# Fourier and MoE kernel on one core: the second transform's fold moved behind its product for the second batch, and its result stores moved from SyncE's queue to ScalarE's

## The chip, the cores and the metric

The kernel runs on one core of a Trainium2 chip. The metric is device time in microseconds (us) of the whole program; what is compared is the median over runs. A profiled execution records every instruction of each engine: PE (TensorE's matmuls), PEld (its weight loads), DVE (VectorE), ACT (ScalarE), POOL (GpSimd), and SPq (the DMA instructions that SyncE issues).

## The reference

Everything is computed on two batches of 3136 rows by 256 columns.

```python
def _attn_ref(x, w_r, w_i, b_r, b_i):
    X = np.fft.rfft(x, axis=1)
    Yr = Xr @ w_r - Xi @ w_i + b_r          # Xr, Xi: real and imaginary part
    Yi = Xr @ w_i + Xi @ w_r + b_i
    # soft threshold by 0.01 on both, then the inverse transform
    return np.fft.irfft(Y, n=x.shape[1], axis=1)

def _moe_ref(x, g_ln, w_ch1, w_ch2):        # 256 -> 1024 -> 256
    xn = (x - mu) / np.sqrt(var + 1e-06) * g_ln
    return x + np.maximum(xn @ w_ch1, 0.0) @ w_ch2

def _moe2_ref(x, w_ch1, w_ch2):
    mixed = np.real(np.fft.fft(np.fft.fft(x, axis=1), axis=2))
    u = x + mixed
    un = (u - mu) / np.sqrt(var + 1e-06)    # no gain
    return u + np.maximum(un @ w_ch1, 0.0) @ w_ch2
```

The kernel's output is `_moe2_ref(_moe_ref(_attn_ref(x)))`.

## The kernel before, in words

Products that need accuracy are made of three passes: each operand is split into a rounded high part and the remainder (low part), and high times high, high times low and low times high are added up in PSUM. Splitting costs a copy (the high part) and a subtraction (the low part) on ACT, DVE or POOL.

**Stages in time.** The first transform and its inverse fill the first part. Then 12 chunks of the first MLP (`mlp1`) run, and then 13 chunks of the second (`mlp2`), each of up to 512 rows. A chunk loads its rows (L591), normalises them (`prep`, L605 to L622: statistics on DVE, and for the chunks that the change touches, the two passes of the normalisation on ACT, four instructions of L621 and four of L622), transposes them on PE (L636 into a `psc` tile), copies them out as high and low part (L641 or L202 on ACT, L642 or L210 on DVE), and then runs two layers. Layer 1 is eight tiles of six matmuls (L220 to L222 into `psa`), each drained by one ACT instruction (L660, the ReLU and high part) and one DVE instruction (L661, the low part); `psa` has 3 buffers. Layer 2 is four tiles of sixteen matmuls (L677, L678 into `psb`, 2 buffers), each drained by two DVE additions (L681, L682) and then stored (L690). PE runs layer 1 of a chunk, then layer 2, with the transposes of the next chunk before the last layer 2 tile.

**The second transform** is the class `Stage98`. It works along the rows of one batch in 16 steps, on a 98x512 piece each. Its object for batch 0, `s4[0]`, is woven into chunks 8 to 10 of `mlp1` (about 350 to 425 us), its object for batch 1, `s4[1]`, into chunks 0 to 3 of `mlp2` (about 492 to 607 us). A step loads a piece that is wanted two steps later (L350), splits another into high and low part, multiplies (L220 to L222 into `psc`, 3 buffers), and copies the result into one of 4 slots of a ring `o98`, from where it is stored to the scratch tensor `dA2` in DRAM (L425). A slot is written again only when its store has landed. `mlp2` reads `dA2` back (L725, L727).

Along the columns the second MLP's transform needs, for each column c and its mirror image, the sum and the difference of the two: the *fold*. For batch 0 the fold is done behind the product: ACT copies columns 0 to 127 out of PSUM (98x256), ACT copies two middle columns from the tile `mid`, and DVE writes difference (L420) and sum (L421). For batch 1 the fold is done ahead of the product, on the loaded piece: three POOL instructions (L369 to L371) write the folded piece `w`, ACT copies its high part `s` (L202, 98x512), POOL subtracts (L210), and after the product ACT copies the whole tile (98x512) and POOL the two middle columns (L424). The loaded pieces lie in a ring `t98` of 2 for batch 0 and in a ring `r98` of 4 for batch 1.

**What sets the order.** The program text gives a priority by position, hooks (`STAGE4_AT`, `STAGE4_MLP2`) say behind which tile of which chunk a step of `Stage98` is written, and a scheduler orders the instructions of each engine with an estimate of when each is ready. On the chip each engine then runs its own list strictly in order, and waits on semaphores at the head. All loads and stores stand in SP's list.

Of the kernel before, what the change touches and what calls it, by code (L numbers as in the profile page):

```python
# [162 lines left out]
def fourier_moe_kernel(ctx, tc, x, w_r, w_i, b_r, b_i, g_ln, w11, w12, w21, w22,  # L163
                       t_ca, t_cam, t_cim, t_cb, t_ci, t_cb0, t_ci0, t_cd, t_ident, out):
    nc = tc.nc
    sp = nc.sync
# [8 lines left out]
    def psum(tag):  # L175
        return pp.tile([128, 512], F32, tag="ps" + tag, name="ps" + tag, bufs=ps_bufs[tag])
# [24 lines left out]
    def a_copy(o, i, scale=1.0):  # L201
        nc.scalar.activation(out=o, in_=i, func=AF.Copy, scale=scale)  # L202
# [15 lines left out]
    def mm3r(ps, lh, ll, rh, rl, first, last):  # L218

        nc.tensor.matmul(out=ps, lhsT=lh, rhs=rh, start=first, stop=False)  # L220
        nc.tensor.matmul(out=ps, lhsT=ll, rhs=rh, start=False, stop=False)  # L221
        ins = nc.tensor.matmul(out=ps, lhsT=lh, rhs=rl, start=False, stop=last)  # L222
        mark["pe"] = getattr(ins, "ins", ins)


    def scratch(nm):
        return [dp.tile([NQ, FW], F32, name=f"{nm}{b}") for b in range(NB)]

    dY, dX1, dA2 = (scratch(n) for n in ("dY", "dX1", "dA2"))
# [48 lines left out]
    class Forward:  # L278


        def __init__(self, b, tag, slot):
            self.b, self.tag, self.slot = b, tag, slot
            self.raw = {}
            self.g = 0
# [10 lines left out]
        def step(self):  # L295
            g = self.g
            if g >= 16:
                return
            e = g % 2
            ps = psum(self.tag)  # L300
            nc.tensor.matmul(out=ps, lhsT=cam, rhs=self.raw[g // 2][:, e * 512:(e + 1) * 512], start=True, stop=True)  # L301
            ins = nc.vector.transpose(out=yg[self.b].rearrange("p k c -> p c k")[:, g * 16:(g + 1) * 16, :],
                                      in_=ps.rearrange("p (c j) -> p c j", j=32))
            mark["dve"] = getattr(ins, "ins", ins)
            self.g += 1
# [28 lines left out]
    class Stage98:  # L334
# [3 lines left out]
        def __init__(self, src, dst, ch, cl, tag):  # L338
            self.src, self.dst, self.ch, self.cl, self.tag = src, dst, ch, cl, tag
            self.raw, self.hl = {}, {}  # L340
            self.fold_last = src is dX1[0]
            self.g = self.nl = self.ns = 0

        def load(self):
# [58 lines left out]
        def step(self):  # L403
            g = self.g
            if g >= 16:
                return
            if g == 0:
                self.middle2()
            self.load()
            self.split()  # L410
            h, l = self.hl.pop(g)
            ps = psum(self.tag)
            mm3r(ps[0:NQ, :], self.ch, self.cl, h, l, True, True)
            o = next(o98_ring)[0:NQ]
            if self.fold_last:
                v, w = (a.rearrange("q (j c) -> q j c", c=D) for a in (ps[0:NQ, :], o))
                a_copy(w[:, :, 0:128], v[:, :, 0:128])
                a_copy(w[:, :, 128], self.mid[:, 2 * g:2 * g + 2])
                lo, hi = w[:, :, 1:128], v[:, :, 255:128:-1]
                nc.vector.tensor_tensor(out=w[:, :, 129:256], in0=lo, in1=hi, op=ALU.subtract)  # L420
                nc.vector.tensor_tensor(out=lo, in0=lo, in1=hi, op=ALU.add)  # L421
            else:
                a_copy(o, ps[0:NQ, :])
                nc.gpsimd.tensor_copy(o[:, 128:512:256], self.mid[:, 2 * g:2 * g + 2])  # L424
            sp.dma_start(out=self.dst[:, g * 512:(g + 1) * 512], in_=o)  # L425
            self.g += 1


# [587 lines left out]
```

## Time and profile before

| what | value |
|---|---|
| median of 3 runs | 822.34 us (822.14 to 823.64) |
| the profiled execution's own time | 823.36 us |
| its span in the profile | 821.5 us |
| granted TensorE clock, share of full speed | 0.998 |
| PE busy | 806.9 us (98%) |
| DVE busy | 534.1 us (65%) |
| ACT busy | 304.5 us (37%) |
| POOL busy | 122.9 us (15%) |

The span is the time from the first to the last recorded instruction; 1.9 us of the execution's own time lie outside it. The profiled execution took 1.02 us more than the median of the runs. A busy share is a mean over stages, so a wait is looked up where it stands, in the timeline of its engine.

In a timeline each row has the start, the time that the instruction (or a row of `xN` like ones) took, the engine, the line, the operation, the tile it writes and the tiles it reads, and in brackets how long the engine had been idle before it and which instruction ended that wait. Successive matmuls overlap in the pipe, so a matmul that is listed with 0.40 us is followed by the next one after about 0.23 us.

### The profile page before, as it was taken

To read this page: it belongs to the slowest core of one execution; us is meant where nothing else is said; L and a number is where in the kernel's file an instruction comes from. 1 tells how busy PE (TensorE), PEld (TensorE's weight loads), DVE (VectorE), ACT (ScalarE), POOL (GpSimd) and SP (SyncE) were. 2 spreads that over 40 slices of the span, in tenths; PEclk is the share of its full clock that TensorE was granted. 3 is DMA by queue.
4 is the path that set the end of the run, shared out by engine and by line. 5 is a ranking of instruction groups with operands and counts; after the bars stand their busy time and mean duration, and the time that the engine had idled before them with its cause. 6 is when DMAs were issued, how large, how long until landed. Compare 5 with 4: busy or idle time off the path is not lost.

```text
span 821.5 us, 12201 instructions
## 1 busy us (share of the span) xinstructions
PE 806.9 (98%) x4456; PEld 674.9 (82%) x4456; DVE 534.1 (65%) x1268; ACT 304.5 (37%) x637; POOL 122.9 (15%) x154
## 2 busy tenths in 40 slices
PE   9999999999999999999999999999999999999996
PEld 3888977967878889978888887888888898888885
DVE  6479996475666588956558655645655667655653
ACT  1422356353344222353442224555632233332221
POOL 1222221211000000045400004635300000000000
PEclk9999999999999999999999999999999999999999
DMA  8742200621015301354333113343232221210001
GB/s 225 217 136 88 78 1 2 214 101 51 2 52 171 118 35 68 123 143 154 98 108 97 63 52 84 118 141 98 90 89 84 58 62 56 65 52 26 20 16 29
DMA packets 48175, 71.57 MB, mean 87 GB/s; under 512 B 11746, under 2 KB 32490, under 8 KB 47920
## 3 DMA queue, kind: packets, MB, share of 16 engines
q1 hardware_dynamic: 48116, 70.80, 28.2%
q8 instruction: 35, 0.57, 0.3%
q14 instruction: 24, 0.20, 0.1%
HBM read 45.09 MB, written 25.69 MB: 86 GB/s over the span
## 4 chain that ended last, share of the span: by engine, by line
PE 85%; DVE 6%; DMA 5%; SPq 1%; POOL 1%; issue 1%; ACT 1%; ACTq 0%; POOLq 0%
PE psb L677 22%; PE psb L678 11%; PE psa L220 11%; PE psa L222 11%; PE psa L221 11%; PE psb L480 4%; PE psc L320 3%; PE psc L741 3%; PE psc L636 3%; PE psc L301 2%; PE psc L500 2%; DMA cb<-in_cb_dram 1%; PE psa L766 1%; PE psa L448 1%; DMA h<-in_x_dram 1%; PE psc L220 1%
## 5 line engine op out<-in xcount | busy, mean ns | idle before, releaser
L660 ACT ACTIVATE h<-psa 128x512 fp32r<-128x512 f32 (+2 forms) x208 | 117.1, 573 | 238.8 <-PE psa L222 213.7
L661 DVE SCALAR_TENSOR_TENSOR h<-psa,h 128x512 fp32r<-128x512 f32 (+2 forms) x208 | 134.4, 654 | 81.6 <-ACT h L660 79.8
L677 PE MATMUL psb<-r2b,h 128*128 128x512 f32 x392 | 138.0, 399 | 0.0
L677 PE MATMUL psb<-r3a,h 128*128 128x512 f32 x392 | 137.6, 399 | 0.0
L678 PE MATMUL psb<-r3a,h 128*128 128x256 f32 x392 | 106.2, 281 | 0.0
L678 PE MATMUL psb<-r2b,h 128*128 128x256 f32 x392 | 105.8, 280 | 0.0
L480 PE MATMUL psb<-wm,h 128*128 128x256 f32 (+1 forms) x600 | 88.8, 298 | 0.7 <-DVE w L486 0.7
L681 DVE TENSOR_TENSOR o<-psb,yb 128x256 f32<-128x256 f32 x74 | 30.1, 422 | 85.9 <-PE psb L678 85.7
L677 PEld LDWEIGHTS psb<-r3a,h 128*128 128x128 f32 x392 | 71.9, 188 | 16.0 <-PE psa L222 0.3
L677 PEld LDWEIGHTS psb<-r2b,h 128*128 128x128 f32 x392 | 71.9, 188 | 15.0
L480 PEld LDWEIGHTS psb<-wm,h 128*128 128x128 f32 (+1 forms) x600 | 76.1, 189 | 8.5 <-issue 8.0
L220 PE MATMUL psa<-q,r3a 128*128 128x512 f32 (+2 forms) x208 | 82.7, 398 | 0.3 <-ACT q L641 0.2
L220 PE MATMUL psa<-q,r2b 128*128 128x512 f32 (+2 forms) x208 | 82.4, 396 | 0.5 <-ACT q L202 0.3
L221 PE MATMUL psa<-q,r3a 128*128 128x512 f32 (+2 forms) x208 | 78.7, 378 | 0.0
L221 PE MATMUL psa<-q,r2b 128*128 128x512 f32 (+2 forms) x208 | 78.5, 378 | 0.0
L222 PE MATMUL psa<-q,r2b 128*128 128x512 f32 (+2 forms) x208 | 78.2, 380 | 0.0
L222 PE MATMUL psa<-q,r3a 128*128 128x512 f32 (+2 forms) x208 | 78.1, 380 | 0.0
L678 PEld LDWEIGHTS psb<-r3a,h 128*128 128x128 f32 x392 | 73.9, 189 | 4.2 <-issue 1.0
L678 PEld LDWEIGHTS psb<-r2b,h 128*128 128x128 f32 x392 | 74.0, 189 | 2.9
L202 ACT ACTIVATE yg<-psc 98x512 f32<-98x512 f32 (+2 forms) x58 | 48.5, 860 | 56.7 <-PE psc L500 27.8
L210 POOL TENSOR_TENSOR h<-w 128x512 f32<-128x512 f32 (+1 forms) x26 | 34.5, 1327 | 109.6 <-DVE w L487 70.4
L220 PEld LDWEIGHTS psa<-q,r3a 128*128 128x128 f32 x208 | 39.1, 188 | 9.5 <-DVE h L661 1.3
(115 smaller groups left out, 1230.9 us busy)
## 6 DMA issues: line engine op xcount, KB each, us to landing
s<-in_moe_w_ch_dram SPq DMA_DIRECT2D x16, 512.0 KB
r<-dX SPq DMA_DIRECT2D x32, 196.0 KB
dA<-o SPq DMA_DIRECT2D x32, 196.0 KB
dY<-yg SPq DMA_DIRECT2D x12, 512.0 KB
r<-dA SPq DMA_DIRECT2D x48, 128.0 KB
dX<-o SPq DMA_DIRECT2D x11, 512.0 KB
yb<-dX SPq DMA_DIRECT2D x50, 64.0 KB
out_dram<-o SPq DMA_DIRECT2D x50, 64.0 KB
```

Of the source, the lines that this page charges most:

```text
L202: nc.scalar.activation(out=o, in_=i, func=AF.Copy, scale=scale)
L210: ins = eng.tensor_tensor(out=o, in0=a, in1=b, op=ALU.subtract)
L220: nc.tensor.matmul(out=ps, lhsT=lh, rhs=rh, start=first, stop=False)
L221: nc.tensor.matmul(out=ps, lhsT=ll, rhs=rh, start=False, stop=False)
L222: ins = nc.tensor.matmul(out=ps, lhsT=lh, rhs=rl, start=False, stop=last)
L320: nc.tensor.matmul(out=ps[0:NQ, :], lhsT=cim, rhs=t, start=True, stop=True)
L480: nc.tensor.matmul(out=ps[0:m, u * D:(u + 1) * D], lhsT=xv[:, o:o + m], rhs=wm_hl[wv][:, e, c, :], start=k == 0, stop=k == 11)
L660: nc.scalar.activation(out=h[:, 0:n], in_=ps[:, 0:n], func=AF.Relu)
L661: ins = nc.vector.scalar_tensor_tensor(out=l[:, 0:n], in0=ps[:, 0:n], scalar=0.0, in1=h[:, 0:n], op0=ALU.max, op1=ALU.subtract)
L677: nc.tensor.matmul(out=ps, lhsT=h[:, ts_], rhs=w2[:, f, :], start=f == 0, stop=False)
L678: nc.tensor.matmul(out=ps[:, 0:D], lhsT=l[:, ts_], rhs=w2[:, f, 0:D], start=False, stop=f == NF - 1)
L681: nc.vector.tensor_tensor(out=o, in0=ps[:, 0:D], in1=self.y[:, i, :], op=ALU.add)
```

## The change

For batch 1 the fold goes behind the product as it is for batch 0 (the flag `fold_last` holds for both objects). With that its load goes to the ring of 2 (`t98`), its split becomes a POOL cast (L361) and a POOL subtraction (L210), and its result is made by ACT's copy of 98x256, ACT's copy of two middle columns, L420 and L421 on DVE. And all 32 result stores (L425), those of batch 0 too, are issued by ACT instead of SP.

```diff
         def __init__(self, src, dst, ch, cl, tag):
             self.src, self.dst, self.ch, self.cl, self.tag = src, dst, ch, cl, tag
             self.raw, self.hl = {}, {}
-            self.fold_last = src is dX1[0]
+            self.fold_last = True
             self.g = self.nl = self.ns = 0
...
                 nc.gpsimd.tensor_copy(o[:, 128:512:256], self.mid[:, 2 * g:2 * g + 2])
-            sp.dma_start(out=self.dst[:, g * 512:(g + 1) * 512], in_=o)
+            nc.scalar.dma_start(out=self.dst[:, g * 512:(g + 1) * 512], in_=o)
             self.g += 1
```

The first place is ACT's list where batch 1 begins, in chunk 0 of `mlp2`. `s` is the high part of a piece, `w` the folded piece that POOL writes, `mid` the middle columns. Before:

```order
L660 ACTIVATE h<-psa 128x512
L202 ACTIVATE s_1657<-w 98x512
L660 ACTIVATE h<-psa 128x512
L202 ACTIVATE s_1657<-w 98x512
L610 ACTIVATE sm<-mv,e_81 128x4
L202 ACTIVATE ng<-mv 128x4
L621 ACTIVATE q<-yb,ng 128x256 x4
L202 ACTIVATE s_1657<-w 98x512
L622 ACTIVATE q<-q,sm 128x256 x4
L202 ACTIVATE mid<-psc 98x32
```

After the change the same place reads:

```order
L660 ACTIVATE h<-psa 128x512 x2
L610 ACTIVATE sm<-mv,e_81 128x4
L202 ACTIVATE ng<-mv 128x4
L621 ACTIVATE q<-yb,ng 128x256 x4
L622 ACTIVATE q<-q,sm 128x256 x4
L202 ACTIVATE mid<-psc 98x32
L202 ACTIVATE o_1658<-mid 98x2 x4
L202 ACTIVATE q<-psc 128x512 x2
```

The three copies `s<-w` between the last ReLUs (L660) of chunk 0 and the normalisation (L621, L622) of chunk 1 are gone from ACT's list, the normalisation follows the ReLUs directly, and four copies of middle columns stand behind `mid`.

The second place is ACT's list in chunk 9 of `mlp1`, where the normalisation of chunk 10 stands among the last ReLUs of chunk 9; `dA_70` is the scratch tensor of batch 0, `o_1658` the ring of 4 slots. Before:

```order
L660 ACTIVATE h<-psa 128x512
L621 ACTIVATE q<-yb,ng 128x256 x4
L660 ACTIVATE h<-psa 128x512
L622 ACTIVATE q<-q,sm 128x256 x4
L660 ACTIVATE h<-psa 128x512
L202 ACTIVATE o_1658<-mid 98x2 x2
L202 ACTIVATE o_1658<-psc 98x2x128
L660 ACTIVATE h<-psa 128x512
L202 ACTIVATE o_1658<-mid 98x2
L202 ACTIVATE o_1658<-psc 98x2x128
```

After the change:

```order
L660 ACTIVATE h<-psa 128x512
L621 ACTIVATE q<-yb,ng 128x256 x4
L425 DMA dA_70<-o_1658 98x512 x2
L660 ACTIVATE h<-psa 128x512
L622 ACTIVATE q<-q,sm 128x256 x4
L660 ACTIVATE h<-psa 128x512
L202 ACTIVATE o_1658<-mid 98x2
L202 ACTIVATE o_1658<-psc 98x2x128
L202 ACTIVATE o_1658<-mid 98x2
L660 ACTIVATE h<-psa 128x512
L425 DMA dA_70<-o_1658 98x512
L202 ACTIVATE o_1658<-mid 98x2
```

Three store issues now stand among these rows, two together ahead of a ReLU (L660) and the third straight ahead of a copy into the ring; before the change they stood in SP's list. Of the two middle copies that stood together, one now stands behind the 98x256 copy. In the whole of ACT's list after the change, 16 of the 29 rows of stores stand straight ahead of an L660 row. PE's list is the same in both kernels up to this chunk, and has the same number of matmuls in all.

## Rows read from the trace of the kernel before

**Rows 1.** The page: the chain that ended last, by engine, share of the span.

```profile
PE 85%; DVE 6%; DMA 5%; SPq 1%; POOL 1%; issue 1%; ACT 1%; ACTq 0%; POOLq 0%
```

**Rows 2.** One stretch: its length, busy PE, PEld, DVE, ACT, POOL (instructions), clock, DMA.

```profile
500.00:550.00 50.00, 48.29 (x266) 40.52 (x265) 24.97 (x62) 26.66 (x60) 24.09 (x40) 1.00 0.40 117
```

**Rows 3.** Timeline of PE from 497 to 506.

```profile
497.04 0.39 PE L222 MATMUL psa<-q,r2b 128*128 128x512 f32 x1
...
502.65 0.40 PE L678 MATMUL psb<-r2b,h 128*128 128x256 f32 x2
504.76 0.44 PE L636 MATMUL psc<-ident,q 128*128 128x128 f32 x2 [1.71 <-ACT q L622]
...
505.75 0.48 PE L677 MATMUL psb<-r2b,h 128*128 128x512 f32 x1
```

**Rows 4.** Timeline of ACT, 496 to 506.

```profile
496.10 0.60 ACT L660 ACTIVATE h<-psa 128x512 fp32r<-128x512 f32 x1 [0.41 <-PE psa L222]
499.40 0.63 ACT L202 ACTIVATE s<-w 98x512 fp32r<-98x512 f32 x1 [2.71 <-POOL w L371]
499.94 0.58 ACT L660 ACTIVATE h<-psa 128x512 fp32r<-128x512 f32 x1
...
501.87 1.71 ACT L621 ACTIVATE q<-yb,ng 128x256 f32<-128x256 f32 x4
503.68 0.63 ACT L202 ACTIVATE s<-w 98x512 fp32r<-98x512 f32 x1
504.21 1.69 ACT L622 ACTIVATE q<-q,sm 128x256 f32<-128x256 f32 x4
```

**Rows 5.** Timeline of POOL, the same stretch.

```profile
497.82 0.73 POOL L369 TENSOR_TENSOR w<-r 98x254 f32<-98x254 f32 x1 [0.53 <-DMA r<-dX]
...
500.83 1.31 POOL L210 TENSOR_TENSOR s<-w,s 98x512 fp32r<-98x512 f32 x1
```

**Rows 6.** Timeline of DVE, the same stretch.

```profile
500.55 0.69 DVE L661 SCALAR_TENSOR_TENSOR h<-psa,h 128x512 fp32r<-128x512 f32 x1 [2.11 <-ACT h L660]
```

**Rows 7.** Timeline of PE, chunk ends at 534 and 594.

```profile
534.63 1.24 PE L636 MATMUL psc<-ident,q 128*128 128x128 f32 x6
535.63 0.48 PE L677 MATMUL psb<-r2b,h 128*128 128x512 f32 x1
...
594.53 1.04 PE L636 MATMUL psc<-ident,q 128*128 128x128 f32 x8
595.32 0.47 PE L677 MATMUL psb<-r2b,h 128*128 128x512 f32 x1
```

**Rows 8.** Instructions on the tile o: count, ns min/median/max, first and last start.

```profile
L202 ACT ACTIVATE o<-psc x32: 364/492/601, 359.1 to 601.9; 98x256 f32<-98x256 f32 x16, 98x512 f32<-98x512 f32 x16
L425 SPq DMA_DIRECT2D dA<-o x32: 307/314/2858, 363.4 to 604.2; - x32
...
L202 ACT ACTIVATE o<-mid x16: 188/202/208, 353.0 to 414.0; 98x2 f32<-98x2 f32 x16
L420 DVE TENSOR_TENSOR o<-o,psc x16: 382/410/422, 361.5 to 422.9; 98x254 f32<-98x254 f32 x16
...
  DMA dA<-o: 15.6, 7
```

**Rows 9.** Timeline of SP around 370 (a store) and 604.

```profile
369.52 0.31 SPq L425 DMA_DIRECT2D dA<-o  x1
...
604.20 2.86 SPq L425 DMA_DIRECT2D dA<-o  x1
```

**Rows 10.** Timeline of ACT around 372.

```profile
371.81 0.21 ACT L202 ACTIVATE o<-mid 98x2 f32<-98x2 f32 x1 [3.40 <-DMA dA<-o]
```

**Rows 11.** Timeline of DVE around 374.

```profile
374.20 0.75 DVE L682 TENSOR_TENSOR o<-psb,o 128x256 f32<-128x256 f32 x2
```

**Rows 12.** Timeline of PE around 374.

```profile
374.76 0.47 PE L677 MATMUL psb<-r3a,h 128*128 128x512 f32 x1
```

**Rows 13.** Timeline of ACT at the end of batch 0's steps.

```profile
417.64 0.60 ACT L660 ACTIVATE h<-psa 128x512 fp32r<-128x512 f32 x1 [1.01 <-PE psa L222]
```

## The prediction

> **What bounds the kernel now.** I read the chain that ended last first: 85% of it is PE, and ACT and POOL together are 2% [rows 1]. So an edit on ACT, POOL, DVE or SP moves the time only where it ends a wait of PE. The second view is busy time by stretch, over the stretches in which batch 1's steps run: PE is busy 48.29 of the 50 us from 500 to 550 [rows 2], so there is one hole of 1.71 us. The third is PE's timeline there: the hole stands whole before the transposes of chunk 1, at 504.76, and was ended by ACT's L622 [rows 3]. Then ACT, POOL and DVE in the same stretch, to see why L622 was late. Last come the instructions on the result tile `o`, whose issues the change moves, and the timelines where they stand on tight places.
>
> **Why L622 is late.** The last tile of layer 1 of chunk 0 was started on PE at 497.04 [rows 3]. ACT should drain it with L660. But ahead of that L660 stands a copy `s<-w`, which waited 2.71 us for POOL's fold [rows 4]; POOL began that fold when the load had landed, at 497.82 [rows 5]. L660 started at 499.94, DVE's L661 behind it had waited 2.11 us and ran at 500.55 [rows 4, 6]. The statistics of chunk 1 stand behind L661, and the normalisation starts at 501.87, that is 1.32 us after L661 did [rows 4, 6]. Between its two passes a third `s<-w` stands: L621 starts at 501.87 and takes 1.71, L622 starts at 504.21, 0.63 of that being the copy [rows 4].
>
> **The fold, step by step.** The three `s<-w` leave ACT's list (first pair of pieces of the order), so L660 can run when its tile is complete, about 497.04 + 0.39 = 497.43 plus a hand-over. I take 497.45 to 498.05 with its 0.60 [rows 4]. DVE's L661 follows from about 498.45, since two statistics instructions of the next chunk stand ahead of it; that is 2.1 us earlier than 500.55. With the same 1.32 us behind it L621 starts at 499.77, L622 at about 501.4, and its first result is there 0.55 us later (504.21 to 504.76), at 501.95. PE comes to the transposes at 504.76 - 1.71 = 503.05. The cover is 1.1 us, and the hole goes: -1.71. What is late next? The fourth L622 ends at 501.4 + 1.69 = 503.1, when PE is only at its first transposes. The split of the first two pieces is two casts (I take half of the subtraction's 1.31 for each) and two subtractions on POOL: 497.82 + 1.3 + 2.6 = 501.7 [rows 5], ahead of the products, which stand behind the transposes. So nothing takes the hole's place.
>
> At two later chunk ends the same copies stand between L621 and L622, and the transposes are stretched without a gap being shown: from their first to the next layer 2 matmul 535.63 - 534.63 = 1.00 us, against 595.32 - 594.53 = 0.79 where there is no `s<-w` left [rows 7]. 564 looks like 534. L622 will start 0.6 us earlier there: -0.21 twice, -0.4.
>
> What the fold adds lies beside PE. DVE gets 32 instructions of 0.41, 13.1 us, over the 100 us in which it was about half busy (24.97 of 50) [rows 2, 8]. ACT's result copy gets shorter (0.36 for 98x256 by the minimum of the row, 0.6 for 98x512 by its maximum) and gains a 0.20 copy, so those two cancel [rows 8]; 16 `s<-w` of 0.63, 10 us, go. POOL loses work and is on no path. I take nothing for these, with -0.3 to +0.6 us as ends. The upper: two fold instructions ahead of the L661 of a late tile make it 0.8 late, most of which three `psa` buffers swallow; I give 0.2 at each of three chunk ends. The lower: ACT's ReLUs come earlier wherever an `s<-w` stood ahead of them, half of the 0.63 at one place where PE waits.
>
> **The stores on ACT.** On SP an issue took 307 to 2858 ns, median 314 [rows 8]. That ACT's issue costs the same is not shown by any row; I take 0.31, with 0 and 2.9 as ends. 32 of them are 10 us more on ACT, as much as the fold takes off it. But an issue waits at the head of ACT's list for DVE's L421, and behind it stand ReLUs: in 16 of 29 places the next row is an L660. On SP behind it stood loads of pieces for the splits, which had time; these get free, and since only POOL waits for them I give nothing for it. Three kinds of place pay:
>
> (a) Chunk 9 (second pair of pieces). Two issues stand ahead of an L660, 0.62 us, and the third, whose turn comes only behind L421, stands straight ahead of a copy into the ring. Before, this store was issued at 369.52 and the copy ran at 371.81, released by the store's landing: 2.29 us [rows 9, 10]. The copy is thus tied to the store, and both move by ACT's delay. Behind the copy come DVE's fold and then its additions; L682 at 374.20 (two, 0.75) hands its `psb` over at about 374.6, and PE's L677 wanted it at 374.76 [rows 11, 12]. So 0.62 less 0.1 of slack: +0.5. Ends: 0 if the issue is hidden, +1.5 if it lands a microsecond later.
>
> (b) The end of batch 0, about 417: three issues ahead of two L660, 0.93 us. ACT idled 1.01 us before the first of them [rows 13], but the issue itself waits for L421, so that idle time is not free for it. I take +0.4, ends 0 and 0.9.
>
> (c) Three chunks of batch 1, each with an issue ahead of a late L660 or a copy behind its own slot's store. I take +0.2 each, +0.6, ends 0 and 3 x 0.9 = 2.7.
>
> The Trainium skill, in DMA: Bandwidth & Descriptors, section "Issuing engines are not separate DMA queues", says that DMAs started from several engines share the same 16 DMA engines, and that a second issuer only saves the sequencer's issue time. By that rule (b) and (c) buy no faster store. The trace agrees as far as it can: ACT waited for landed stores only 15.6 us in 7 places, and the one at 371.81 ended by landing, not by a late issue [rows 8, 10].
>
> Sum: 823.36 - 1.71 - 0.4 + 0.5 + 0.4 + 0.6 = 822.75 us for an execution like the profiled one. That was 1.02 us above the median of 822.34, so 821.7 in the terms of the median, 0.6 us under it. A change within 0.2%, 1.64 us or 820.7 to 824.0, can't be told from none here.
>
> **Rivals.** A, faster: an issue from ACT costs its list next to nothing. For it: most issues on SP are short, and 10 us of copies leave ACT where it was tightest. Against it: waiting for L421 is left even with a free issue, and (a) keeps its copy behind the landing. Terms (a) to (c) shrink to 0.2: 822.34 - 2.11 + 0.2 = 820.4 us.
>
> B, slower: ACT's issues are held up as SP's are behind a burst of loads. At 604.20 a store took 2.86 us to issue [rows 9], and SP is still bursting at the chunk ends where batch 1's stores stand. On SP nobody waited; on ACT an L660 stands behind, whose slack is that of `psa`: 3 buffers of 6 matmuls of 0.23 are 4.1 us, less the running tile (1.4), L660 (0.60) and L661 (0.69), so about 1.4. An issue of 2.86 passes it by 1.5. Four chunk ends with one such issue each cost 6 us, at half that excess 3 us; with the 1.5 of the sum: 822.34 - 2.1 + 1.5 + 3 to 6 = 824.7 to 827.7, I take 825.5. It decides from issues of about 1.4 us alone, or 0.7 where two stand together. Against it: the median of the row is 0.31, and (a) and (b) lie where SP issues little.
> The Trainium skill's Perfetto Trace Analysis, section "DMA Instruction — HWDGE (DVE, Sync)", has one descriptor generator shared by the two issuing sequencers, and the issue's profiled time with the wait for its lock in it. By that rule ACT's issues are held while SP issues, which is B at 825.5; the trace has stores from one issuer only and can't show it, the 2.86 row bears it out in part.
>
> C, the hole stays: L622 is late for another reason, since the load itself landed as late as 497.82 and might be later with the ring of 2. Then -0.4 + 1.5: 823.4. Against it: in the new list nothing ahead of L622 reads that piece.
>
> **How the numbers follow.** Forecast 0.47, own range 820.5 to 823.5; A 0.25; B 0.18; C 0.10. Faster by over 0.2% is A and a little of the forecast's low end, 0.28. Slower is B and the high end of C, 0.20. The rest, 0.52, is within. The range leaves out the best of A and the worst of B: 819.8 to 825.2.
>
> **What the new profile would show.** Right: no row of PE waiting for L622 near 504, the transposes at 534 and 564 taking 0.79, ACT's issues at 0.3, PE waits of 0.2 to 0.6 for L660, L661 or L682 near 374, 418 and at batch 1's chunk ends. Wrong: issues on ACT of over 1 us with PE waits for DVE's L661 behind them (B), no waits there at all (A), or the hole still at 504 (C).

## The result and the profile after

The changed kernel took 831.9 us (median of 4 runs, 831.58 to 833.59) where the kernel before took 822.99 (4 runs): a ratio of 1.010 with an interval of 1.0083 to 1.0117. It is slower by 8.9 us between the medians, clear of the noise, and outside the range of the prediction. The profiled execution took 831.82 us with a span of 830.0, against 821.5 before: 8.5 us more.

TensorE's waits come first. Each row has who waited for whom, the total, how often, and the longest.

```profile
PE psa L220 <- DVE h L661: 6.9, 4, 2.7
```

Before, TensorE had no such row; its longest wait was for L622 [rows 3]. Those four waits stand in its timeline:

```profile
395.60 0.50 PE L220 MATMUL psa<-q,r3a 128*128 128x512 f32 x1 [0.62 <-DVE h L661]
...
526.55 0.79 PE L220 MATMUL psa<-q,r2b 128*128 128x512 f32 x1 [2.19 <-DVE h L661]
...
560.43 0.62 PE L220 MATMUL psa<-q,r2b 128*128 128x512 f32 x1 [2.72 <-DVE h L661]
...
592.96 0.50 PE L220 MATMUL psa<-q,r2b 128*128 128x512 f32 x1 [1.35 <-DVE h L661]
```

One is in batch 0's stretch, and one in each of the chunks 1 to 3 of the second MLP, where batch 1's steps run. The hole at 504 is gone, as forecast: the transposes follow the last layer 2 matmul at once. At the next chunk end eight transposes now stand together and take 0.80 us:

```profile
504.17 0.40 PE L678 MATMUL psb<-r2b,h 128*128 128x256 f32 x2
504.41 0.38 PE L636 MATMUL psc<-ident,q 128*128 128x128 f32 x2
...
537.96 1.04 PE L636 MATMUL psc<-ident,q 128*128 128x128 f32 x8
538.76 0.48 PE L677 MATMUL psb<-r2b,h 128*128 128x512 f32 x1
```

Before, the 1.00 us there were for six of them [rows 7]. The other two stood 3 us later, ahead of the next layer 2 tile:

```profile
538.54 0.38 PE L636 MATMUL psc<-ident,q 128*128 128x128 f32 x2
538.67 0.48 PE L677 MATMUL psb<-r2b,h 128*128 128x512 f32 x1
```

With their 0.13 us the eight took 1.13, so the gain is 0.3 us; at the chunk end after it it is the same.

What holds L661 at 526 is read from ScalarE's timeline:

```profile
517.80 0.39 ACT L202 ACTIVATE o<-psc 98x256 f32<-98x256 f32 x1
520.26 0.31 ACTq L425 DMA_DIRECT2D dA<-o  x1
520.62 0.60 ACT L660 ACTIVATE h<-psa 128x512 fp32r<-128x512 f32 x1 [2.44 <-PE psa L766]
...
521.77 0.41 ACT L202 ACTIVATE o<-psc 98x256 f32<-98x256 f32 x1
525.08 0.20 ACT L202 ACTIVATE o<-mid 98x2 f32<-98x2 f32 x1 [2.90 <-DMA dA<-o]
525.17 0.32 ACTq L425 DMA_DIRECT2D dA<-o  x1
525.19 1.06 ACT L660 ACTIVATE h<-psa 128x512 fp32r<-128x512 f32 x2
529.17 0.20 ACT L202 ACTIVATE o<-mid 98x2 f32<-98x2 f32 x1 [2.91 <-DMA dA<-o]
```

and from VectorE's:

```profile
522.75 0.41 DVE L421 TENSOR_TENSOR o<-o,psc 98x254 f32<-98x254 f32 x1
...
525.80 0.69 DVE L661 SCALAR_TENSOR_TENSOR h<-psa,h 128x512 fp32r<-128x512 f32 x1 [1.64 <-ACT h L660]
```

At 522.18 ScalarE is done with its copy out of PSUM and comes to a copy of two middle columns, `o<-mid`, for a later step. This copy is to write into the ring slot whose store was issued at 520.26, and waits until that has landed, at 525.08: 4.8 us after the issue. Behind it in the list stand two ReLUs (L660), one of which TensorE's next layer 1 tile needs drained, and the store of the step whose L421 began at 522.75. That store goes out at 525.17, 2.0 us after L421 ended, and so the next middle copy waits again until 529.17. A copy of 0.20 us holds ScalarE, the ReLU, L661 behind it, and TensorE.

The rows of the result tile sum it up:

```profile
L425 ACTq DMA_DIRECT2D dA<-o x32: 314/314/675, 364.1 to 611.7; - x32
...
  DMA dA<-o: 46.5, 18
```

An issue on ScalarE costs 314 ns in the median and 675 at the most, as SyncE's median and far from its 2858 [rows 8]. Waits for landed stores rose from 15.6 us in 7 places [rows 8] to 46.5 in 18.

The waits cost more than they last. These are layer 1 matmuls behind the wait of 2.19, then the stretch of the slow matmuls and one behind it (length, busy PE, PEld, DVE, ACT, POOL, clock, DMA):

```profile
527.14 0.63 PE L221 MATMUL psa<-q,r2b 128*128 128x512 f32 x1
527.57 0.63 PE L222 MATMUL psa<-q,r2b 128*128 128x512 f32 x1
...
529.70 0.51 PE L221 MATMUL psa<-q,r2b 128*128 128x512 f32 x1
530.05 0.40 PE L222 MATMUL psa<-q,r2b 128*128 128x512 f32 x1
530.28 0.39 PE L220 MATMUL psa<-q,r2b 128*128 128x512 f32 x1
```

```profile
526.53:529.94 3.41, 3.39 (x8) 2.72 (x9) 1.38 (x7) 0.77 (x4) 0.00 (x0) 0.50 0.33 107
...
532.00:536.00 4.00, 4.00 (x24) 3.37 (x23) 2.64 (x10) 2.71 (x9) 1.91 (x2) 1.00 0.01 2
```

From one start to the next they take 0.43 us, and 0.23 again from 530.05 on: behind the wait the granted clock is at 0.50, the lower level of 1.2 GHz, and then at 1.00 again. From 526.55 to 530.05 that is 3.50 us for eight intervals, where 8 x 0.23 = 1.84 are due: 1.7 us. Behind the wait of 2.72 the same: eight intervals from 560.43 to 563.84, then 0.34, 1.7 us again. Behind the wait of 1.35 the clock stayed at 1.00.

The sum of the two profiles: waits for L661 of 2.19 + 2.72 + 1.35 + 0.62 = +6.9, slow clock +3.4, the hole -1.7, the transposes twice -0.3; that makes +8.0 of the 8.5 us between the spans. Another 0.6 is TensorE's wait near 355 for a cast on POOL (L361), 0.60 us before and 1.19 after. That wait takes 0.4 to 1.3 us over the ten kernels of this document, so it is not put down to the change.

### The profile page after: what moved, and what is told of

It reads as the page before. It is cut to its first block, busy times and chain, and to the rows that moved or that the text cites. A ratio compares the mean times of both kernels' runs of the same rounds, so it can differ in the third digit from the quotient of the medians.

```text
span 830.0 us, 12194 instructions
## 1 busy us (share of the span) xinstructions
PE 808.8 (97%) x4456; PEld 676.9 (82%) x4456; DVE 544.9 (66%) x1300; ACT 294.5 (35%) x637; POOL 104.3 (13%) x106
## 5 line engine op out<-in xcount | busy, mean ns | idle before, releaser
L660 ACT ACTIVATE h<-psa 128x512 fp32r<-128x512 f32 (+2 forms) x208 | 117.0, 572 | 230.5 <-PE psa L222 205.9
L661 DVE SCALAR_TENSOR_TENSOR h<-psa,h 128x512 fp32r<-128x512 f32 (+2 forms) x208 | 134.5, 653 | 76.9 <-ACT h L660 75.5
L220 PE MATMUL psa<-q,r2b 128*128 128x512 f32 (+2 forms) x208 | 83.8, 403 | 6.7 <-DVE h L661 6.3
L221 PE MATMUL psa<-q,r2b 128*128 128x512 f32 (+2 forms) x208 | 79.8, 385 | 0.0
L222 PE MATMUL psa<-q,r2b 128*128 128x512 f32 (+2 forms) x208 | 79.3, 384 | 0.0
L220 PEld LDWEIGHTS psa<-q,r2b 128*128 128x128 f32 x208 | 39.9, 192 | 15.7 <-DVE h L661 7.7
L210 POOL TENSOR_TENSOR h<-w 128x512 f32<-128x512 f32 (+1 forms) x26 | 34.4, 1326 | 109.1 <-DVE w L487 69.5
```

What stands on the lines that cost most here:

```text
L210: ins = eng.tensor_tensor(out=o, in0=a, in1=b, op=ALU.subtract)
L660: nc.scalar.activation(out=h[:, 0:n], in_=ps[:, 0:n], func=AF.Relu)
L661: ins = nc.vector.scalar_tensor_tensor(out=l[:, 0:n], in0=ps[:, 0:n], scalar=0.0, in1=h[:, 0:n], op0=ALU.max, op1=ALU.subtract)
```

## The experiments

Two theories stood at first. M: the middle copies, which the new fold puts on ScalarE, wait there for landings. Q: the stores in ScalarE's list are the cause. The comparisons were made later than the result above, in two sessions; the kernel before took 826.19 us beside the first four kernels (13 runs) and 824.83 beside the last four (15 runs), so ratios are given. The changed kernel was not timed again beside them; its 1.010 is from the result above.

**The fold alone** (the changed kernel with its stores back on SyncE's queue):

```diff
-            nc.scalar.dma_start(out=self.dst[:, g * 512:(g + 1) * 512], in_=o)
+            sp.dma_start(out=self.dst[:, g * 512:(g + 1) * 512], in_=o)
```

> The fold moved as in the change, the stores left on SyncE's queue. Theory M (the two-column copies from mid, which the new fold puts on ScalarE, wait there for the landing of the store that last used their ring slot, and hold the ReLUs of layer 1 behind them): the copies are still on ScalarE, so TensorE still waits for L661 in the chunks of batch 1, in all 3 to 8 us, and the time is 826 to 832. Theory Q (the stores are the cause: in ScalarE's list they are issued late and land late): the hole at 504 goes and nothing comes in its place, 820 to 822.

Measured: 841.78 us, ratio 1.0199 (1.0172 to 1.0226). Theory M had the sign and the place, but the size is beyond it: twice the loss of the whole change. ScalarE's timeline has two middle copies in a row with longer waits (the second is the one that stood until 525.08 in the changed kernel), and TensorE's has the stall behind them:

```profile
517.11 0.20 ACT L202 ACTIVATE o<-mid 98x2 f32<-98x2 f32 x1 [10.08 <-DMA dA<-o]
...
527.94 0.20 ACT L202 ACTIVATE o<-mid 98x2 f32<-98x2 f32 x1 [5.45 <-DMA dA<-o]
```

```profile
529.41 0.79 PE L220 MATMUL psa<-q,r2b 128*128 128x512 f32 x1 [4.41 <-DVE h L661]
```

```profile
PE psa L220 <- DVE h L661: 12.6, 4, 4.4
...
560.14:566.97 6.83, 5.81 (x15) 4.65 (x16) 5.43 (x15) 3.05 (x10) 1.90 (x2) 0.50 0.51 149
```

The sum closes here too. TensorE's waits for L661 are 12.6 us, and the clock is at 0.50 in three stretches of 3.4, 6.8 and 3.4 us, of which 1.0 lies within a wait: 6.3 us lost. Less 1.7 and 0.6 that makes 16.6 of the 17.1 us between the spans. So the second half of the change did not cause the loss: with it the ratio is 1.010, and TensorE's waits for L661 are 6.9 us in place of 12.6.

**The stores alone** (the kernel before with only line 425 changed):

```diff
-            sp.dma_start(out=self.dst[:, g * 512:(g + 1) * 512], in_=o)
+            nc.scalar.dma_start(out=self.dst[:, g * 512:(g + 1) * 512], in_=o)
```

> The stores on ScalarE's queue, the fold of batch 1 left ahead of its product (so its middle columns are copied by GpSimd). Theory M: no copy of batch 1 on ScalarE waits early for a ring slot, TensorE's waits of 1.3 to 2.7 us before L220 near 526, 560 and 593 are gone, the hole of 1.7 us at 504 is back, 822 to 825. Theory Q: the stores alone bring the loss, TensorE waits for L661 as in the changed kernel, 828 to 833.

Measured: 826.91 us, ratio 1.0006 (0.9995 to 1.0017). Nothing either way, and TensorE has no wait for L661; theory Q is out. (Theory M's 825 was meant for a kernel before of 822 us; here that took 826.19.) The hole is back:

```profile
507.53 0.44 PE L636 MATMUL psc<-ident,q 128*128 128x128 f32 x2 [2.25 <-ACT q L622]
```

**The whole change, middle columns by GpSimd:**

```diff
-                a_copy(w[:, :, 128], self.mid[:, 2 * g:2 * g + 2])
+                nc.gpsimd.tensor_copy(w[:, :, 128], self.mid[:, 2 * g:2 * g + 2])
```

> The whole change, but the copy of the two middle columns runs on GpSimd for both batches. ScalarE still issues the stores and still writes each result slot with its copy out of PSUM, which stands behind the product. Theory M: the waits before L220 near 526, 560 and 593 go, 820 to 823. Theory Q: stores still late on ScalarE, 828 or more.

Measured: 822.8 us, ratio 0.9954 (0.9939 to 0.9968), 3.8 us under the kernel before. TensorE's order of matmuls is the same as in the changed kernel; the edit moves only a 0.2 us copy to another engine. In the waits of this kernel the landings are still waited for, by GpSimd now:

```profile
POOL o L418 <- DMA dA<-o: 40.4, 17, 4.8
```

That is 40.4 us in 17 places beside 46.5 in 18, and no wait of TensorE is put down to them. Of TensorE's four waits for L661 one is left:

```profile
525.40 0.50 PE L220 MATMUL psa<-q,r2b 128*128 128x512 f32 x1 [0.72 <-DVE h L661]
```

**The whole change, result ring of 8 slots instead of 4:**

```diff
-    s98_ring = ring(cp.tile([128, S98 * 512], F32R, tag="u0", name="s98"), S98, 512)
-    o98_ring = ring(cp.tile([128, O98 * 512], F32, tag="wm", name="o98"), O98, 512)
+    so98 = cp.tile([128, 16 * 512], F32R, tag="u0", name="s98")
+    s98_ring = ring(so98[:, 0:S98 * 512], S98, 512)
+    o98_ring = ring(so98[:, S98 * 512:16 * 512], 8, 512)
```

> [...] A slot is written again 8 steps after its store, so no copy on ScalarE waits for a landing. Theory M: ScalarE's waits for the landing of stores fall from 46.5 us to below 5, 820 to 823. Theory Q: the stores' place in ScalarE's list is unchanged, TensorE's waits stay, 828 or more.

Measured: 831.16 us, ratio 1.0058 (1.0043 to 1.0073): less than the whole change's 1.010, but more than half of the loss stays. Theory M's expectation is missed: ScalarE's waits for landings fall only from 46.5 to 31.5 us, and TensorE still waits for L661, 5.5 us in 3 places. Theory Q expected waits like these, and 828 or more, but the stores alone cost nothing. ScalarE's waits and its timeline (in this kernel the ring carries the name `s`):

```profile
ACT s L202 <- DMA dA<-s: 31.5, 11, 5.1
...
521.60 0.41 ACT L202 ACTIVATE s<-psc 98x256 fp32r<-98x256 f32 x1
525.25 0.20 ACT L202 ACTIVATE s<-mid 98x2 fp32r<-98x2 f32 x1 [3.24 <-DMA dA<-s]
525.33 0.32 ACTq L425 DMA_DIRECT2D dA<-s  x1
525.36 1.07 ACT L660 ACTIVATE h<-psa 128x512 fp32r<-128x512 f32 x2
```

The same wait at the same place. In the list of this kernel eight middle copies stand in a row behind batch 0's `mid` instead of four, and then again one behind nearly every store. A middle copy needs only `mid`, which is there from the start, and a free slot. So it is placed where a slot is estimated to come free, be it for the step four or eight ahead; a deeper ring lets it run further ahead and leaves it behind the latest store. That gave theory H: not the depth of the ring but the early place of the copy is the cause. The next two kernels test it, with the copy left on ScalarE.

**The whole change, each middle copy tied behind the copy out of PSUM of its own step:**

```diff
-                a_copy(w[:, :, 0:128], v[:, :, 0:128])
-                a_copy(w[:, :, 128], self.mid[:, 2 * g:2 * g + 2])
+                ins = nc.scalar.activation(out=w[:, :, 0:128], in_=v[:, :, 0:128], func=AF.Copy)
+                with tc.issue_after(getattr(ins, "ins", ins)):
+                    a_copy(w[:, :, 128], self.mid[:, 2 * g:2 * g + 2])
```

> The whole change with the ring of 4 and the middle columns still copied by ScalarE, but each such copy tied behind the copy out of PSUM of its own step (one line more, so the line numbers behind it are one higher). The ring of 8 showed that more slots do not end the waits. Theory H (the early place in ScalarE's list is the cause, whatever the depth: the copy stands where its slot was estimated to come free, ahead of ReLUs that are ready): TensorE's waits of 1.3 to 2.7 us before L220 go, 820 to 823 where the kernel before has 822.3, a ratio of 0.995 to 1.000. Theory E (any copy from mid on ScalarE costs, since ScalarE is too full): 826 or more, ratio over 1.004.

Measured: 822.46 us, ratio 0.9966 (0.9953 to 0.9979). Theory H. ScalarE at the place of the stall, every line number one higher:

```profile
522.34 0.41 ACT L417 ACTIVATE o<-psc 98x256 f32<-98x256 f32 x1
522.60 0.23 ACT L202 ACTIVATE o<-mid 98x2 f32<-98x2 f32 x1
523.03 0.60 ACT L661 ACTIVATE h<-psa 128x512 fp32r<-128x512 f32 x1 [0.20 <-PE psa L222]
```

ScalarE's list has no wait of a middle copy for a landing left: the copy stands behind the product, and by then its slot has been stored. The ReLU waits 0.20 us for TensorE and not TensorE for it. A small wait stays, as with GpSimd's copies:

```profile
525.37 0.50 PE L220 MATMUL psa<-q,r2b 128*128 128x512 f32 x1 [0.57 <-DVE h L662]
```

**The fold alone, with tied copies** (both edits together):

> The same tied copies, with the stores on SyncE's queue. Theory H: the waits that made the fold alone 16 us slower go, ratio 0.994 to 1.000. Theory S (with the stores on SyncE the fold is slow by itself, since a store stands in SyncE's list behind loads and output stores, and its slot comes free late for any writer): ratio over 1.005, with TensorE waiting for L661 as in the fold alone.

Measured: 822.51 us, ratio 0.9969 (0.9953 to 0.9984). From 1.0199 to this by tying 32 copies of 0.2 us. Between 490 and 620 TensorE's timeline shows no wait at all, not the 0.57 either.

**The fold alone, middle columns by GpSimd** (the stores on SyncE):

> Fold for both batches, stores on SyncE's queue, middle columns copied by GpSimd. Theory H: as fast as the same with ScalarE's stores, ratio 0.994 to 0.998; the store's queue is worth under 1 us once no early copy waits on ScalarE. Theory S: ratio over 1.002, the copies out of PSUM on ScalarE wait for late stores instead.

Measured: 821.56 us, ratio 0.9961 (0.9946 to 0.9977). GpSimd's wait in this kernel is nearly that of the fold alone, 60.3 us in 16 places on ScalarE there:

```profile
POOL o L418 <- DMA dA<-o: 58.3, 15, 8.2
```

With either cure the queue of the stores can't be told: 0.9954 and 0.9966 with ScalarE's, 0.9961 and 0.9969 with SyncE's, all intervals overlapping. Theory S falls.

**The kernel before, batch 0's middle columns by GpSimd:**

> The kernel before with only the middle columns of batch 0 copied by GpSimd instead of ScalarE. It shows what the early copies cost batch 0 already. Theory H predicts little, since TensorE had no wait for L661 there: ratio 0.998 to 1.001, the hole of 1.7 us at 504 unchanged. If the copies of batch 0 held something after all, the ratio is below 0.997.

Measured: 826.19 us, ratio 1.0021 (1.0003 to 1.0038): no gain, rather a small loss, a little above theory H's range. The hole stays, here a little longer than 1.71, and behind it the clock is lower in this execution (1.00 at the hole before):

```profile
505.31 0.61 PE L636 MATMUL psc<-ident,q 128*128 128x128 f32 x2 [2.12 <-ACT q L622]
```

```profile
501.00:510.00 9.00, 6.88 (x35) 5.99 (x35) 3.34 (x11) 5.01 (x14) 5.64 (x8) 0.81 0.35 99
```

So batch 0's early copies, with stores on SyncE, cost nothing that their removal gives back. The loss needs the copies in batch 1's stretch.

## Why the prediction was wrong

**The hole: right. The transposes: the sign right, the size misread.** -1.71 came as worked out. The 0.2 at each later chunk end compared 1.00 us for six transposes with 0.79 for eight [rows 7]; all eight had taken 1.13, and 0.3 was gained. The four kernels without early copies show the gain: 0.3 to 0.5%, that is 2.6 to 3.8 us, where these terms make 2.3. The rest may be the clock: its mean over the runs was 0.998 in each of the four, and 0.996 and 0.997 in the kernel before beside them. No trace of the kernel before from those sessions shows it.

**The issue's cost: right.** 0.31 was taken and 0.314 measured. Rival B, the one rival priced as slower, had its sign by chance: no issue on ScalarE reached its 1.4 us; the longest was 675 ns. While SyncE issued four loads, from 519.47 to 522.22, ScalarE's store at 520.26 took its 0.31:

```profile
519.47 2.75 SPq L725 DMA_DIRECT2D r<-dA  x4
```

The section of the Trainium skill that the prediction put beside B (Perfetto Trace Analysis, "DMA Instruction — HWDGE (DVE, Sync)") gives the shared descriptor generator to DVE and SyncE and does not speak of ScalarE; no hold of that kind shows on ScalarE's issues here.

**Terms (a) and (b): too dear.** TensorE shows no wait near 374 or 418. One of 0.62 came at 395 in their place, which no step named; it is gone with the middle columns on GpSimd, in the same order of matmuls.

**The failed step is term (c), and the line "those two cancel" above it.** The fold's middle copy was costed by its 0.20 us of work and set against a shorter copy. Its wait was not costed where it mattered. The prediction had the row that shows the mechanism: at 371.81 such a copy stood 3.40 us for a landing [rows 10]. It was used for one place of batch 0; for batch 1, where the change puts 16 of these copies onto ScalarE among ReLUs, "a copy behind its own slot's store" got 0.2 us a chunk, and 0.9 at the most. Measured were 2.19, 2.72 and 1.35, and 3.4 for the clock behind two of them: 9.7 us where 0.6 stood. Three things made it so. The order had the copies straight behind stores with ReLUs behind them, and that was not followed from store to store. The landing was taken as 2.29 us [rows 9, 10], while in batch 1's stretch it was 4.8 (520.26 to 525.08) and 4.0 (525.17 to 529.17). And a blocked copy holds the next store too, which then holds the next copy.

The Trainium skill, in DMA: Bandwidth & Descriptors, section "Latency and other measured facts", puts a DMA's fixed cost at about 2 us. The 2.29, a whole landing, is near it; the 4.0 and 4.8 are not. In the trace a landing shows as updates of the store's semaphore, fifteen for each of these stores. Of the store at 520.26 thirteen had come 2.60 us behind the issue, and the last two at 4.76 and 4.79; of the one at 525.17 thirteen by 2.27, and the last two at 3.88 and 3.98. SyncE was issuing loads around both (of `dA2` from 519.47, of `dX1` from 522.32), but that these held the last two back was not tested.

**The clock was left out.** Before the change the wait of 1.71 at 504 stood in a stretch with the clock at 1.00 [rows 2, 3], and the prediction gave every new wait its length and nothing more; in the changed kernel those of 2.19 and 2.72 cost 1.7 us each on top.

**The range** rested on every bound being small by itself. That waits in one in-order list feed each other was in no bound.

The store at 520.26 went out 1.06 us after its L421 had ended (518.78 + 0.42 = 519.20), and the trace shows why. It waits for two semaphores: that of L421, updated at 519.21, and the one that it signals itself, on which a store of an output tile by SyncE still counted:

```profile
513.13 1.14 SPq L690 DMA_DIRECT2D out_dram<-o  x2
```

That one's last updates came at 520.12 and 520.17, and ScalarE's wait ended at 520.19. What stays open is whether this makes the 0.6 to 0.7 us of wait near 525 which the cured kernels show with stores on ScalarE and not with stores on SyncE; no run tried it without.

## What to carry to other kernels

Cost an instruction that joins an in-order engine by what it waits for at its place in the list, and by what stands behind it there, not by its own duration. A tiny copy whose data is ready early and whose target is a ring slot was scheduled here straight behind the store that frees the slot; put it on an idle engine, or tie it behind the instruction that truly needs the slot. A ring of 8 slots in place of 4 did not cure that, and the wait that moved to GpSimd (40 us) shows in no wait of TensorE.

## What was not expected of the hardware

A store's landing, as seen by the instruction that waits for its slot, took from 2.3 to 5.1 us within one chunk of the changed kernel:

```profile
553.87 0.32 ACTq L425 DMA_DIRECT2D dA<-o  x1
...
558.97 0.20 ACT L202 ACTIVATE o<-mid 98x2 f32<-98x2 f32 x1 [3.18 <-DMA dA<-o]
559.03 0.31 ACTq L425 DMA_DIRECT2D dA<-o  x1
...
561.33 0.20 ACT L202 ACTIVATE o<-mid 98x2 f32<-98x2 f32 x1 [1.19 <-DMA dA<-o]
```

The first copy waited for the first store, 5.1 us behind its issue, the second for the second, 2.3 us behind. Of the first store's fifteen updates thirteen had come by 2.54 us, and the last two came at 4.93 and 5.07; of the second's all had come by 2.27.

And the waits of TensorE that the profiles show in the second MLP of 2.12, 2.19, 2.25, 2.59, 2.70, 2.72, 3.79, 3.92 and 4.41 us, in five kernels, each went with a stretch at the lower clock level; those of 1.35 and 1.71 us did not.
